# Pairs of chunks as the unit of decay in a linear-attention kernel: states summed in PSUM, weights cast on the way in, k scaled on GpSimd, r copied by stepped PSUM reads

## The chip, the cores and the metric

The kernel runs on one core of a Trainium2 chip. The metric is the device time of one execution in microseconds: 207.22 us for the kernel before (median of 2 runs, 206.41 and 208.04). The profile is of one execution, with a span of 204.4 us from its first to its last instruction.

The core's engines run side by side, each through its own queue in order: TensorE (PE in the profile; PEld is its weight load), VectorE (DVE), ScalarE (ACT), GpSimd (POOL) and SyncE (SP), which here only issues transfers. TensorE writes to PSUM, of which there are eight banks of 512 float32 per partition. VectorE and ScalarE read PSUM and SBUF[...].

## What is computed

Two phases follow each other: a linear attention with per-channel decay, and a token- and channel-mixing block on its output.

```python
# B, H, S, D = 4, 8, 768, 48
for t in range(S):
    kt, vt, rt = k[:, :, t], v[:, :, t], r[:, :, t]
    cur = einsum('bhd,bhe->bhde', u[None] * kt, vt)
    y[:, :, t] = einsum('bhd,bhde->bhe', rt, state + cur)
    state = w[None, :, :, None] * state + einsum('bhd,bhe->bhde', kt, vt)
x = y.transpose(0, 2, 1, 3).reshape(B, S, H * D)      # 4, 768, 384

theta = x @ w_theta
yr = einsum('ts,bsd->btd', w_tok_r, x * cos(theta))
yi = einsum('ts,bsd->btd', w_tok_i, x * sin(theta))
u = x + yr + yi
out = u + maximum(u @ w_ch, 0)
```

## The kernel before

**Chunks.** The 768 tokens of a batch are six chunks of 128 (C), taken in three pairs (`pr`). Within a chunk the decay is put into the operands: r is multiplied by w to a power that rises with the token's place in its chunk (`wpow`), k by one that falls with it (`wpinv`). Then the scores of a chunk are a plain product of k and r, masked to the part below the diagonal, and the state that enters the next chunk is the old state plus the chunk's k-v product, times w to the 128th power (`wC`). The heads go two by two (`hp`, four pairs), each padded from 48 to 64 channels, so that two heads fill 128 partitions.

**`front(b)`** does the attention of a batch and the way to cos and sin.
- r arrives with six consecutive tokens per partition. L397 scales it into `Rw` (GpSimd; for batch 0 two of four head pairs on VectorE). `flip6` transposes six 128x128 blocks into one PSUM bank (L379, TensorE) and ScalarE copies the bank to SBUF as `RT` (L382). Because of the six tokens per partition the copy reads the bank in a row and writes at a step of six elements, so that the tokens come out in order.
- k of a pair of chunks is scaled by VectorE into `Kw` (L416) and transposed to `KT` (L379, L382). v is cast by ScalarE into `vb` (L424).
- Scores of a chunk (L438) fill two banks, one per head of a pair. VectorE masks each into `mAT` (L443). The diagonal with u goes through `PD` (L449), a small product (L459), `dg` (L464) and GpSimd's `yd` (L466).
- The k-v products of the first five chunks (L479) go to PSUM. VectorE adds each to the decayed earlier state, head pair by head pair, into `Y` (L494; a copy for the first, L491), and GpSimd multiplies by `wC` into the bf16 state `Sb` (L499). Both of a chunk's steps hang on the chunk before.
- `outputs` adds state times r (L516) and masked scores times v (L526); VectorE adds `yd` into `x` (L535). x is transposed, multiplied by theta's weights (L552), goes through sin and cos on ScalarE (L556, L559), and becomes `zr` (VectorE, L562) and `zi` (GpSimd, L565).

**`mixing(b)`** multiplies zr and zi of all six chunks by the token weights (twelve matmuls of 384 columns per 128 tokens, L586), adds x (L592), transposes, multiplies by the channel weights (L604), ends with a maximum and an addition (L609) and stores.

**Weights.** Wth and Wch come as float32 and are cast by ScalarE (`square`, L347). Each of twelve row blocks of the token weights comes as float32, is transposed by TensorE in float32, three blocks to a bank (L361), and copied as bf16 by ScalarE (L367). All their transfers, like those of r, k and v, are issued by SyncE, and all but r land in a ring of eight buffers (`ld`). In that queue the weights stand between batch 0's k and v and batch 1's r.

**The order.** Nothing is ordered by hand. `Plan.add` records each step with its engine, an assumed duration, a priority, what it reads and writes and which PSUM banks it takes and gives back. `Plan.order` (L72) plays the list through as a small simulation: at each moment a free engine takes the ready task of the lowest priority number for which banks are free. The kernel is then issued in that order, so assumed durations and priorities fix both the order in each queue and the bank that each result gets. Mixing of a batch has a higher number than the next batch's front, so it fills TensorE's time while the front waits.

Of the kernel before, what the change touches and what calls it, by code (L numbers as in the profile page):

```python
# [19 lines left out]


# [6 lines left out]
PE, DVE, ACT, POOL, SP = "PE", "DVE", "ACT", "POOL", "SP"  # L28


class Task:
    __slots__ = ("eng", "ns", "fn", "deps", "prio", "seq", "lat", "acq", "uses", "nwait",
                 "users", "ready", "end", "mode")


class Plan:
# [3 lines left out]
    def __init__(self, nbanks):  # L40
        self.tasks, self.writer, self.readers = [], {}, {}
        self.nbanks = nbanks
        self.bank_uses = {}
        self.bank_of = {}

    def add(self, eng, ns, fn, rd=(), wr=(), prio=0.0, lat=60.0, acq=(), use=(), mode=None):
        t = Task()
        t.eng, t.ns, t.fn, t.prio, t.lat, t.mode = eng, ns, fn, prio, lat, mode
        t.seq = len(self.tasks)
        t.acq, t.uses = list(acq), list(acq) + list(use)  # L50
        rd, wr = list(rd) + list(use), list(wr) + list(acq)
# [19 lines left out]

    def order(self):  # L72
# [11 lines left out]
        banks = [(0.0, i) for i in range(self.nbanks)]  # L84
# [3 lines left out]
        while len(out) < n:  # L88
            for e in waiting:
                while free_at[e] <= now:  # L90
                    nfree = sum(1 for b in banks if b[0] <= now)
                    best = None
                    for t in waiting[e]:
                        if t.ready <= now and len(t.acq) <= nfree:
                            if best is None or (t.prio, t.seq) < (best.prio, best.seq):
                                best = t
# [4 lines left out]
                    banks.sort()  # L101
                    for b in t.acq:
                        self.bank_of[b] = banks.pop(0)[1]
                    ns = t.ns
                    if e == PE:
                        if t.mode != last_mode:
                            ns += 100.0
                        last_mode = t.mode
                    free_at[e] = now + ns
                    t.end = now + ns + t.lat  # L110
                    out.append(t)
                    for b in t.uses:
                        left[b] -= 1
                        freed[b] = max(freed.get(b, 0.0), t.end)
                        if left[b] == 0:
                            banks.append((freed[b], self.bank_of[b]))
# [7 lines left out]
            nxt += [b[0] for b in banks if b[0] > now]  # L124
# [3 lines left out]
            now = min(nxt)  # L128
        return out


def rows_of(w, n):
    return dataclasses.replace(w, ap=[[0, n]] + [list(x) for x in w.ap])


def wide(ap, n):
    return dataclasses.replace(ap, ap=[list(x) for x in ap.ap] + [[0, n]])
# [3 lines left out]
def kernel(  # L141
# [22 lines left out]
    NS = NCH - 1  # L164
# [4 lines left out]
    bank_t = [ps.tile([C, 512], F32, name=f"bank{i}") for i in range(8)]  # L169

    def bank(tok):
        return bank_t[P.bank_of[tok]]
# [6 lines left out]

# [9 lines left out]
    tok_i = sb.tile([C, NCH + 1], mybir.dt.int32, name="tok_i")  # L189
    tok_f = sb.tile([C, NCH + 1], F32, name="tok_f")  # L190
    wpow = sb.tile([C, H, NCH, D], F32, name="wpow")
    wpinv = sb.tile([C, H, D], F32, name="wpinv")
    wup = sb.tile([C, 2 * HP], F32, name="wup")
    wC = sb.tile([C, HP], F32, name="wC")
    uw = sb.tile([C, HP, 2], BF16, name="uw")

    NL = 8
    Ls = ring(NL, [C, 2 * HD], F32, "ld")
    r_fs = ring(2, [C, H, NCH * D], F32, "r_f")
    Rws = ring(1, [C, NCH, H, Dp], BF16, "Rw")  # L200
    Kws = ring(4, [C, 2, H, Dp], BF16, "Kw")
    vbs = ring(5, [C, 2, H, D], BF16, "vb")
# [3 lines left out]
    mATs = ring(6, [C, 2, HP, C], BF16, "mAT")  # L206
    Ys = ring(1, [C, NS, HP, D], F32, "Y")
    Sbs = ring(2, [C, NS, HP, D], BF16, "Sb")
    dgs = ring(3, [C, 2 * H], F32, "dg")
# [6 lines left out]
    uns = ring(2, [C, 2, HD], BF16, "un")  # L216
# [3 lines left out]
    Wch = sb.tile([C, ND, HD], BF16, name="Wch")  # L220
    WrT = sb.tile([C, NCH, S], BF16, name="WrT")
    WiT = sb.tile([C, NCH, S], BF16, name="WiT")

    def act_ns(n, psum=True):
        return n / 1.2 + (60 if psum else 95)

    def dve_ns(n, rate=1.0):
        return n / (0.96 * rate) + 75

    def pool_ns(n):  # L230
        return 190 + 1.95 * n


    def setup():
        P.add(ACT, 100, lambda: nc.scalar.dma_start(out=w_f, in_=rows_of(w, C)),
              wr=["w_f"], prio=-100, lat=3000)
# [3 lines left out]
        P.add(DVE, 100, wu_fill, wr=["wu"], prio=-100)  # L240

        def wu_load():
            nc.scalar.dma_start(out=wu[:HP, :, :D], in_=w.rearrange("(a b) d -> a b d", b=2))
            nc.scalar.dma_start(out=wu[HP:, :, :D], in_=u.rearrange("(a b) d -> a b d", b=2))
        P.add(ACT, 200, wu_load, wr=["wu"], prio=-99, lat=3000)

        def tok():
            nc.gpsimd.iota(tok_i[:, :NCH], pattern=[[1, NCH]], base=0, channel_multiplier=NCH)
            nc.gpsimd.iota(tok_i[:, NCH:], pattern=[[0, 1]], base=0, channel_multiplier=1)
        P.add(POOL, 400, tok, wr=["tok_i"], prio=-100)  # L250

        def tok2():
            nc.vector.tensor_scalar(tok_i[:, :NCH], tok_i[:, :NCH], C - 1, None,
                                    op0=Alu.bitwise_and)
            nc.vector.tensor_copy(tok_f, tok_i)
            nc.vector.tensor_scalar(tok_f[:, NCH:], tok_f[:, NCH:], -1.0, -1.0,
# [3 lines left out]
        P.add(DVE, 400, tok2, rd=["tok_i"], wr=["tok_f", "uw", "pi2"], prio=-99)  # L260

        def pads(ts):
            for t in ts:
                nc.gpsimd.memset(t[:, :, :, D:], 0.0)
        P.add(POOL, 900, lambda: make_identity(nc, ident_f), wr=["ident_f"], prio=-98)
        P.add(DVE, 200, lambda: nc.vector.tensor_copy(ident, ident_f), rd=["ident_f"],
              wr=["ident"], prio=-98)
        P.add(POOL, 600, lambda: pads(Rws), wr=[("Rw", hp) for hp in range(HP)], prio=-97)
        P.add(POOL, 800, lambda: pads(Kws), wr=[("Kw", i) for i in range(4)], prio=-96)
# [6 lines left out]
        P.add(POOL, 600, mask, wr=["mask"], prio=-95)  # L276
# [383 lines left out]
```

## Time and profile before

| | busy us | share of span | instructions |
|---|---|---|---|
| TensorE matmul | 145.3 | 71% | 1641 |
| VectorE | 124.6 | 61% | 260 |
| ScalarE | 123.3 | 60% | 165 |
| GpSimd | 75.1 | 37% | 73 |

Sums of a line's busy time, in us, for the lines that the change touches:

| line | what | count | us |
|---|---|---|---|
| L382, ACT | all copies after `flip6`, RT (16) among them | 52 | 72.5 |
| L367, ACT | copies of token weights | 24 | 10.2 |
| L397, POOL | r times `wpow` | 14 | 22.7 |
| L416, DVE | k times `wpinv` | 24 | 21.7 |
| L443, DVE | masks | 48 | 30.6 |
| L494, DVE | state update | 80 | 12.5 |
| L499, POOL | state times `wC` | 20 | 11.5 |
| L361, PE | float32 transposes of token weights | 72 | 10.0 |
| L586, PE | token mixing | 288 | 57.9 |

In the profile "RT_104<-bank_65 128x768 bf16<-128x768 bf16" means that the instruction wrote RT, read a PSUM bank, and moved 768 elements on each of 128 partitions. A bracket with an arrow gives the idle time of the engine just before, and what ended it. A busy share is an average over stages with different limits; which engine a stage waits for is read from the stage. TensorE's clock is granted by a throttle and is below full speed in part of the span (mean 0.921).

### The profile page before, as it was taken

The numbers are of one execution on the slowest core, as the hardware profiler recorded it, in microseconds if no ns is written. First come the engines' busy times: TensorE is split into PE (matmuls) and PEld (weight loads), VectorE is DVE, ScalarE is ACT, GpSimd is POOL, SyncE is SP. The second block draws the span as 40 slices with busy tenths as digits, with TensorE's granted clock in tenths as the row PEclk, the third lists the DMA queues.
The fourth block names the chain that finished last, engine by engine and source line by source line (L and its number), as shares of the span: only waits on it lengthen the run. The fifth ranks groups of instructions, "written<-read, shape, count | busy, mean of one in ns | idle before, by whom it ended". The sixth has DMA issues, their size and how long they took to land.

```text
span 204.4 us, 4137 instructions
## 1 busy us (share of the span) xinstructions
PE 145.3 (71%) x1641; PEld 95.7 (47%) x1641; DVE 124.6 (61%) x260; ACT 123.3 (60%) x165; POOL 75.1 (37%) x73
## 2 busy tenths in 40 slices
PE   0008178896582897599933988999329989999971
PEld 0016165774460555356621755657215655566630
DVE  2028279355740899978861999944419896544442
ACT  2299987999599706409999433755992327511120
POOL 6024121606960489523791083440104082400000
PEclk9999999999669589969995899999985999999998
DMA  4999209999899992829290510022020002022222
GB/s 119 236 230 227 112 6 275 333 332 321 170 198 292 189 167 50 263 69 203 81 195 0 129 29 3 0 82 77 0 77 3 0 3 77 3 77 77 79 80 77
DMA packets 60092, 25.25 MB, mean 124 GB/s; under 512 B 50472, under 2 KB 58536, under 8 KB 60072
## 3 DMA queue, kind: packets, MB, share of 16 engines
q1 hardware_dynamic: 59904, 24.78, 49.9%
q8 instruction: 13, 0.21, 0.5%
q10 hardware_dynamic: 168, 0.20, 0.5%
q14 instruction: 7, 0.06, 0.1%
HBM read 20.25 MB, written 4.72 MB: 122 GB/s over the span
## 4 chain that ended last, share of the span: by engine, by line
PE 41%; ACT 21%; DVE 19%; issue 8%; DMA 8%; POOL 1%; ACTq 0%; POOLq 0%; DVEq 0%; SPq 0%
ACT RT_104 L382 8%; ACT RT_105 L382 7%; DMA r_f_93<-in_r_dram 5%; PE bank_66 L586 5%; PE bank_64 L586 3%; DMA wu<-in_u_dram 3%; PE bank_68 L586 2%; PE bank_63 L586 2%; PE bank_65 L586 2%; DVE Y_116 L494 2%; DVE mAT_114 L443 2%; ACT wpow L297 2%; PE bank_67 L586 1%; PE bank_62 L586 1%; DVE Kw_96 L416 1%
## 5 line engine op out<-in xcount | busy, mean ns | idle before, releaser
L586 PEld LDWEIGHTS <-WrT 128*128 128x128 bf16 x144 | 14.5, 104 | 10.4 <-issue 3.1
L499 POOL TENSOR_TENSOR Sb_118<-Y_116,wC 128x192 bf16<-128x192 f32 x10 | 5.4, 544 | 34.0 <-DVE Y_116 L494 18.6
L586 PEld LDWEIGHTS <-WiT 128*128 128x128 bf16 x144 | 12.8, 98 | 6.8 <-issue 0.5
L397 POOL TENSOR_TENSOR Rw_94<-r_f_92,wpow 128x576 bf16<-128x576 f32 x6 | 10.1, 1713 | 10.1 <-ACT wpow L297 10.1
L397 POOL TENSOR_TENSOR Rw_94<-r_f_93,wpow 128x576 bf16<-128x576 f32 x8 | 12.6, 1600 | 0.4 <-DMA r_f_93<-in_r_dram 0.4
L499 POOL TENSOR_TENSOR Sb_117<-Y_116,wC 128x192 bf16<-128x192 f32 x10 | 6.1, 606 | 16.6 <-DVE Y_116 L494 13.5
L379 PEld LDWEIGHTS <-Rw_94 128*128 128x128 bf16 x96 | 8.0, 120 | 8.6 <-issue 6.2
L438 PEld LDWEIGHTS <-KT_107 64*128 64x128 bf16 x96 | 4.1, 116 | 12.4 <-issue 8.1
L449 DVE TENSOR_TENSOR PD_109<-RT_105,KT_107 128x1024 bf16<-128x1024 bf16 x4 | 3.3, 823 | 10.8 <-ACT RT_105 L382 6.6
L449 DVE TENSOR_TENSOR PD_108<-RT_104,KT_106 128x1024 bf16<-128x1024 bf16 x4 | 4.1, 1030 | 6.8 <-ACT KT_106 L382 6.8
L382 ACT ACTIVATE xT_135<-bank_65 128x768 bf16<-128x768 bf16 x2 | 1.6, 810 | 11.0 <-PE bank_65 L379 11.0
L438 PEld LDWEIGHTS <-KT_106 64*128 64x128 bf16 x96 | 3.8, 117 | 8.6 <-ACT KT_106 L382 5.9
L604 PEld LDWEIGHTS <-uT_138 128*128 128x128 bf16 x36 | 3.5, 108 | 8.9 <-ACT uT_138 L382 6.4
L282 PE MATMUL bank_61<-ident_f,wu 8*128 8x8 f32 x1 | 0.2, 239 | 8.7 <-DMA wu<-in_u_dram 8.7
L604 PEld LDWEIGHTS <-uT_139 128*128 128x128 bf16 x36 | 3.2, 98 | 7.0 <-ACT uT_139 L382 5.3
L382 ACT ACTIVATE RT_104<-bank_65 128x768 bf16<-128x768 bf16 x2 | 5.7, 2844 | 0.4 <-PE bank_65 L379 0.4
L382 ACT ACTIVATE RT_104<-bank_63 128x768 bf16<-128x768 bf16 x2 | 5.9, 2946 | 0.0
L382 ACT ACTIVATE RT_105<-bank_66 128x768 bf16<-128x768 bf16 x2 | 5.7, 2842 | 0.1
L604 PE MATMUL bank_68<-Wch,uT_138 128*128 128x384 bf16 x6 | 1.8, 424 | 5.3 <-ACT uT_138 L382 5.3
L379 PE MATMUL bank_62<-ident,Rw_94 128*128 128x128 bf16 x12 | 1.3, 261 | 5.8 <-DVE Rw_94 L397 5.8
L552 PEld LDWEIGHTS <-xT_134 128*128 128x128 bf16 x36 | 3.5, 106 | 4.1 <-ACT xT_134 L382 2.0
L438 PE MATMUL bank_61<-RT_104,KT_106 64*128 64x128 bf16 x12 | 1.4, 246 | 5.6 <-ACT KT_106 L382 5.6
(540 smaller groups left out, 542.3 us busy)
## 6 DMA issues: line engine op xcount, KB each, us to landing
r_f_92<-in_r_dram SPq DMA_DIRECT2D x2, 1152.0 KB, 7.8
r_f_93<-in_r_dram SPq DMA_DIRECT2D x2, 1152.0 KB, 10.4
out_dram<-fin_140 SPq DMA_DIRECT2D x6, 384.0 KB, 2.4
out_dram<-fin_141 SPq DMA_DIRECT2D x6, 384.0 KB, 2.4
ld_88<-in_k_dram SPq DMA_DIRECT2D x4, 192.0 KB, 6.6
ld_89<-in_v_dram SPq DMA_DIRECT2D x4, 192.0 KB, 3.3
ld_84<-in_k_dram SPq DMA_DIRECT2D x4, 192.0 KB, 5.6
ld_87<-in_moe_w_tok_i_dram SPq DMA_DIRECT2D x2, 384.0 KB, 4.6
```

The costliest lines, as they stand in the source:

```text
L297: P.add(ACT, 500 + (1300 if n == 0 else 0), lambda n=n: nc.scalar.activation(wpow[:, :, n, :], lw_f, Act.Exp, scale=tok_f[:, n:n + 1]), rd ...
L379: nc.tensor.matmul(bank16(tok)[:, i * C:(i + 1) * C], s, ident, is_transpose=True, start=(i == 0), stop=(i == n - 1))
L382: P.add(ACT, act_ns(n * C), lambda: nc.scalar.activation(dst, bank16(tok)[:, :n * C].rearrange("p (a c) -> p a c", a=n), Act.Copy), use=[t ...
L397: eng.tensor_mul(Rw[:, :, 2 * hp:2 * hp + 2, :D].transpose([0, 2, 1, 3]), rf[:, 2 * hp:2 * hp + 2, :].rearrange("p h (n d) -> p h n d", n= ...
L438: nc.tensor.matmul(bank(tk[hi])[:, hp * C:(hp + 1) * C], KT[q, c, hp, :], RT[q, hp, cc * C:(cc + 1) * C], start=(hp == 0), stop=(hp == HP ...
L443: P.add(DVE, dve_ns(HP * C), lambda hi=hi, tk=tk, mAT=mAT: nc.vector.tensor_mul(mAT[:, hi], bank(tk[hi]).rearrange("p (h t) -> p h t", h=H ...
L449: nc.vector.tensor_mul(PD, RT[:, :, 2 * pr * C:(2 * pr + 2) * C].rearrange("p h (a t) -> p a h t", a=2), KT)
L494: nc.vector.scalar_tensor_tensor(Y[:, cc, hp, :], Y[:, cc - 1, hp, :], wC[:, hp:hp + 1], src[:, hp], op0=Alu.mult, op1=Alu.add)
L499: P.add(POOL, pool_ns(HP * D), lambda cc=cc: nc.gpsimd.tensor_mul(Sb[:, cc], Y[:, cc], wide(wC, D)), rd=[("Y", cc), "wC"], wr=[("Sb", b % ...
L552: nc.tensor.matmul(bank(th)[:, :HD], xT[:, t, dk, :], Wth[:, dk, :], start=(dk == 0), stop=(dk == ND - 1))
L586: nc.tensor.matmul(bank(tm)[:, :HD], WT[:, so, to * C:(to + 1) * C], z[:, so], start=(part == 0 and j == 0), stop=(part == 3 and j == 2))
L604: nc.tensor.matmul(bank(tf)[:, :HD], uT[:, t, dk, :], Wch[:, dk, :], start=(dk == 0), stop=(dk == ND - 1))
```

## The change

**Decay relative to pairs.** r's power now runs over a pair of chunks (place in the pair minus 128, `wr_t`) and k's likewise (127 minus the place, `wk_t`, one table per chunk of the pair). So the k-v products of a pair's two chunks need no decay between them and add up in PSUM: TensorE forms the first chunk's product (for the state in the middle of the pair) and, beside it, the sum of both (for the state after the pair), at the price of computing the first one twice. VectorE adds the carried state for the middle (`mid`) and for the end (`carry`), over all heads at once. The decay by w to the 256th (`wP`) falls due once per pair: in the first pair on VectorE, in the second on GpSimd (`decay`); ScalarE makes the bf16 copy. It shortens the chain from chunk to chunk.

**r's copies.** `flip6` gets a `view`: ScalarE reads the bank at a step of 128 elements and writes RT in a row. It is meant to move the step from the write to the read.

**k on GpSimd**, chunk by chunk, to relieve VectorE. **Weights cast by their transfer**: issued by GpSimd, they arrive as bf16, in `Wth`, `Wch` and a ring of six row buffers, and are transposed in bf16, six blocks to a bank. ScalarE's casts fall away, and SyncE's queue and ring hold only r, k, v (rings of six chunks each) and the outputs.

**Smaller things.** The PSUM is four tiles of two banks, and scores take an aligned pair of banks, so one mask instruction covers 1024 elements. Ln and exp share one table, loaded early; sin's is loaded early as well. exp no longer waits for the small loads of w and u, which SyncE now issues. The planner's assumed durations are different, and it models the transfers and pairs of banks. Some rings have other sizes (Kw 3, vb 4, mAT 5, un 3).

```diff
+    bank_t = [ps.tile([C, 1024], F32, name=f"bank{i}") for i in range(4)]
...
+        P.add(ACT, 1300, lambda: nc.scalar.preload_act_table_set("natural_log_exp_and_others"),
+              wr=["tab"], prio=-99.5, name="tab")
...
+                P.add(POOL, 1000, lambda row=row, src=src, to=to: nc.gpsimd.dma_start(
+                    out=row, in_=src[to * C:(to + 1) * C, :]), wr=[rk],
+                    prio=prio + to, dma=1100, name=key)
+                flip6(dst[:, :, to * C:(to + 1) * C], [row[:, j * C:(j + 1) * C] for j in range(NCH)],
+                      ("W", key, to), prio + 30 + to, [rk], [(key, to)])
...
-            flip6(RT[:, hp].rearrange("q (p n) -> q n p", n=NCH),
-                  [Rw[:, n, 2 * hp:2 * hp + 2, :] for n in range(NCH)],
-                  ("TR", b, hp), base + hp, [("Rw", hp)], [("RT", b % 2, hp)])
+            flip6(RT[:, hp], [Rw[:, n, 2 * hp:2 * hp + 2, :] for n in range(NCH)],
+                  ("TR", b, hp), base + hp, [("Rw", hp)], [("RT", b % 2, hp)],
+                  view=lambda s: s.rearrange("q (n p) -> q p n", n=NCH))
...
+                P.add(POOL, pool_ns(384, 2.0), lambda c=c, Kw=Kw, ik=ik: nc.gpsimd.tensor_mul(
+                    Kw[:, c, :, :D], lk[ik], wk_t[:, c]),
+                    rd=[("lk", ik), ("wk_t", c)], wr=[kK[c]], prio=pb, name=f"scale_k{b}.{cc}")
...
+                todo = [(0, 0)] if last else [(0, 0), (1, 0), (1, 1)]
+                for a, c in todo:
...
+                            o = (a * HP + hp) * D
                             nc.tensor.matmul(
                                 bank(ts)[hi * Dp:(hi + 1) * Dp, o:o + D], Kw[:, c, h, :],
...
+                    nc.vector.tensor_add(Sb[:, c1], src, Cf[pr % 2])
...
+                        nc.vector.tensor_add(Yf[0][:, 0], src, Cf[pr % 2])
...
+                    P.add(POOL, pool_ns(HP * D), lambda pr=pr: nc.gpsimd.tensor_mul(
+                        Cf[(pr + 1) % 2], Yf[0][:, 0], wide(wP, D)),
```

## The prediction

> **What bounds the kernel now.** I read the page's busy shares and slices first, then the chain, then one window table cut at the places where the chain showed ScalarE, then ScalarE's timeline in one such place, and last the waits of the SyncE queue.
>
> The busy shares, the slices and the chain (on the page; in the slices each digit is a fortieth of the span, 5.1 us):
>
> ```profile
> PE 145.3 (71%) x1641; PEld 95.7 (47%) x1641; DVE 124.6 (61%) x260; ACT 123.3 (60%) x165; POOL 75.1 (37%) x73
> PE   0008178896582897599933988999329989999971
> ACT  2299987999599706409999433755992327511120
> PEclk9999999999669589969995899999985999999998
> GB/s 119 236 230 227 112 6 275 333 332 321 170 198 292 189 167 50 263 69 203 81 195 0 129 29 3 0 82 77 0 77 3 0 3 77 3 77 77 79 80 77
> ...
> ACT RT_104 L382 8%; ACT RT_105 L382 7%; DMA r_f_93<-in_r_dram 5%; PE bank_66 L586 5%; PE bank_64 L586 3%; DMA wu<-in_u_dram 3%; PE bank_68 L586 2%; PE bank_63 L586 2%; PE bank_65 L586 2%; DVE Y_116 L494 2%; DVE mAT_114 L443 2%; ACT wpow L297 2%; PE bank_67 L586 1%; PE bank_62 L586 1%; DVE Kw_96 L416 1%
> ```
>
> TensorE has the most work and is yet idle 204.4 - 145.3 = 59.1 us. Its row dips where ScalarE's is at 9, and its clock digits fall to 5 or 6 near those dips. The chain's two heaviest entries are the copies of the transposed r out of PSUM, RT at L382. The window table puts a number on them. Columns are length, then busy time (and instructions) of PE, PEld, DVE, ACT, POOL, then clock, DMA share and GB/s. The first four rows are the four batches' RT copies, the other four are what lies between them:
>
> ```profile
> 15.00:27.00 12.00, 5.47 (x58) 4.11 (x58) 5.83 (x11) 11.56 (x7) 3.83 (x4) 1.00 0.68 153
> 56.00:67.00 11.00, 5.74 (x44) 3.86 (x43) 2.29 (x4) 11.00 (x10) 3.77 (x3) 0.81 1.17 243
> 99.50:110.00 10.50, 4.06 (x77) 3.32 (x75) 6.15 (x12) 10.50 (x5) 8.27 (x7) 0.87 0.72 131
> 142.50:152.00 9.50, 2.48 (x49) 1.70 (x46) 2.17 (x7) 9.50 (x6) 1.01 (x2) 0.98 0.11 41
> 27.00:56.00 29.00, 23.05 (x310) 18.15 (x311) 20.28 (x41) 24.25 (x48) 13.43 (x11) 0.94 0.87 252
> 67.00:99.50 32.50, 28.63 (x331) 17.66 (x331) 29.52 (x61) 16.21 (x30) 18.29 (x15) 0.85 0.75 145
> 110.00:142.50 32.50, 29.95 (x352) 19.35 (x352) 25.40 (x53) 17.45 (x28) 11.23 (x9) 0.94 0.18 50
> 152.00:204.40 52.40, 45.47 (x428) 27.21 (x428) 30.03 (x63) 15.30 (x27) 11.17 (x9) 0.92 0.12 46
> ```
>
> In the first four ScalarE is full and TensorE idle 6.5 + 5.3 + 6.4 + 7.0 = 25.2 us of 43. In the other four TensorE is idle 6.0 + 3.9 + 2.5 + 6.9 = 19.3 us of 146; before 15 us it does almost nothing. ScalarE's timeline in the third window (start, length) shows why:
>
> ```profile
> 99.31 2.78 ACT L382 ACTIVATE RT_104<-bank_65 128x768 bf16<-128x768 bf16 x1 [0.45 <-PE bank_65 L379]
> 101.70 2.98 ACT L382 ACTIVATE RT_104<-bank_66 128x768 bf16<-128x768 bf16 x1
> 104.29 2.95 ACT L382 ACTIVATE RT_104<-bank_61 128x768 bf16<-128x768 bf16 x1
> 106.85 2.94 ACT L382 ACTIVATE RT_104<-bank_63 128x768 bf16<-128x768 bf16 x1
> 109.40 1.03 ACT L382 ACTIVATE uT_138<-bank_64 128x768 bf16<-128x768 bf16 x1
> ```
>
> uT has the same line, shape and type and takes 1.03 us here, others of that form 0.81. The difference is that RT is written at a step of six elements. And the SyncE queue:
>
> ```profile
> SPq L324 <- ACT Wth L347: 10.2, 1, 10.2
> ```
>
> For 10.2 us a load waits for a landing buffer that ScalarE empties (the theta weights, whose cast stands behind RT). This is the 6 in the GB/s row, slice 6: DMA stands still at 25 to 30 us, and batch 1's r, last in that queue, lands at 51.5.
>
> **What the Trainium skill says.** "ScalarE: Activation LUTs", section "What ACT_TABLE_LOAD costs": an element per cycle whatever the function, 0.833 ns, plus 186 ns per instruction. For 768 elements that is 0.83 us; the trace's 0.81 agrees, and RT at 2.75 to 2.98 does not, so the stepped write is the anomaly. "SBUF — State Buffer", section "Door 1": 16-byte lines in SBUF and 8-byte lines in PSUM, a penalty for crossing; RT's step of 12 bytes fits that for the write, and the changed copy steps 256 bytes in PSUM, for which the page names only matmuls as slowed. No row of before shows a stepped PSUM read. "TensorE: Matmul & The Clock Gate", section "HAM oscillation — how this bites in real kernels": idle gaps over about 3.4 us put TensorE back to a slow clock. The trace agrees: after the RT windows three mixing matmuls take 0.98 to 1.14 us, elsewhere 0.49. "SBUF — State Buffer", section "Who interferes with whom": a VectorE instruction with two SBUF inputs contends with a GpSimd one that reads SBUF. L416 agrees: 0.55 us alone, 1.29 to 1.76 beside the GpSimd scaling of r.
>
> **The change, part by part.**
> RT's 16 copies now read PSUM stepped and write in a row. Bounds: 0.81 us (same shape, in a row both ways) and about 2.85 (if a step costs as much on the read side). I take 0.85, since the per-element figure is for the engine and the slow part here is the two-byte stepped write. ScalarE loses 16 x 2.0 = 32 us, a batch's burst goes from 11.4 to 3.4 us. Of the 25.2 us of TensorE idle in the four windows some 5 stay, because transposes and copies still alternate: -20 us.
>
> Clock. The 288 mixing matmuls take 57.9 us in sum, theta 14.7 and chan 15.5 (72 each). At 0.163 us apiece (0.49 for three) they need 47.0 + 11.7 + 11.7, so 17.7 us are slow clock and lone starts. Fewer long gaps should give back about half: -8.
>
> Head. exp no longer waits for the tiny w and u loads (8.7 us) and a second table load: it began at 10.74 and can follow Ln at 7.65, so 3.1 us earlier. Weights leave the SyncE queue and its landing ring, so the 10.2 us wait is gone and r of batch 1 follows the 12 k and v loads directly. Against that stand the GpSimd's own duties: seven casting loads stand in its queue ahead of the first scaling of r, and k's scaling follows. A casting load's issue time is in no row of before; the lower bound is what SyncE shows, 0.33 us; "DMA: Bandwidth & Descriptors", section "Latency and other measured facts", prices this path at about 1 us to the first byte, the descriptors being made in software. I take 1 and keep 2, its double, as the upper end. So GpSimd is ready at 3.9 + 7 = 10.9, just as exp is done. The loads of batch 0 also share the DMA with 2.9 MB of weights. r (1.2 MB), w (0.2), twelve loads of 0.2 and those weights make 6.7 MB; at the 230 GB/s of slices 2 to 4 that is 29 us, so the last k and v land at about 29, as now (the last v is issued at 29.4). The gain is in what follows: batch 0's last zi ended at 60.1 and should end at about 45. Much of this is the first RT window again, counted above: -4 beyond it.
>
> VectorE. k's 24 multiplies (21.7 us in sum) go to GpSimd. The state update, 16 x 4 small instructions (12.5 us) and four copies (1.4), becomes 12 + 8 of about 0.28 = 5.6. 48 mask multiplies of 0.64 become 24 of about 1.15, half the starts: -3. In all 124.6 - 21.7 - 8.3 - 3 = 92 us. It was the last to end in 74 to 86 us (k beside r): -2.
>
> GpSimd. 75.1 - 11.5 (20 state scalings) + 2.3 (four remain) + 24 k scalings + 14 issues. 192 elements take 0.51, 768 take 1.47: 1.67 ns each, so 384 take 0.83 to 1.1 us, 23 in sum. Total 103 us. It stays below TensorE, but what stands in its queue is now on the way of every front: behind a casting load that waits for its row buffer stand zi and the next batch's k, and KT's transpose waits for these.
>
> TensorE. 72 float32 transposes (9.97 us) become 72 of bf16 at 0.0915 (30.7 / 336) = 6.6; 64 more state products at 0.035 (5.58 / 160) = 2.2. Net -1.2.
>
> Small: ScalarE no longer casts weights (2.8 us) and copies eight states (8 x 0.26), hidden beside TensorE. The two-bank PSUM tiles add no wait of a half for the other, as the order of instructions and waits shows. Scores need a free pair of banks, which costs nothing while masks keep up.
>
> Sum: 204.4 - 20 - 8 - 4 - 2 - 1.2 = 169.2 us of span; the stated time lies 207.2 - 204.4 = 2.8 above the span: 172 us.
>
> **The rivals.**
> Everything packs. TensorE keeps its clock and the fronts hide: 145.3 - 17.7 - 1.2 = 126 of work, 14 of head, 6 of tail (190 to 204 has 5.6 idle), 10 between: 156 + 3 = 159. For it: 170 to 190 us of before is full at a clock of 1.0. Against: only one stretch is so.
>
> GpSimd and the shared DMA take the place of the waits removed. With issue at 2 us, the first scaling starts 7 us later, the six loads of the second half cost 6 more in the middle of batch 1's front, of which half is seen: 172 + 7 + 3 = 182. For it: seven issues ahead of the first useful GpSimd work, and 6 to 10 us from issue to landing in the crowded head. Against: GpSimd idles 63% now.
>
> The stepped read costs what the stepped write did. Then the 20 and 8 stay away: 204.4 - 4 - 2 - 1.2 = 197 + 3 = 200, or about 195 with the DMA hole gone. For it: no row shows such a read. Against: ScalarE is the engine that reads an element per cycle in every other row.
>
> Slower. A stepped read twice as slow as the write adds 11.4 us to each of the four bursts, of which TensorE hides half: 200 + 23 = 223. It needs a cost of 5.7 us for 768 elements, seven times the plain one.
>
> **How the numbers follow.** Forecast 0.56, everything packs 0.08, GpSimd and DMA 0.22, stepped read 0.09, slower 0.05. The likeliest is 172. From 158 to 190 the first three are inside with their scatter, and about 0.16 is left out. Faster by over 2% is below 203: 0.56 + 0.08 + 0.22 and half of the stepped read, 0.05: 0.91. Within 2%: 0.04. Slower: 0.05.
>
> **What would show it.** RT rows of 0.8 to 1.0 us at the new L393; no window with ScalarE full and TensorE under half; no slices at clock 5 or 6 after the head; mixing near 50 us in sum; the last zi of batch 0 near 45 us; no wait of SyncE for a weight cast; VectorE near 92 and GpSimd near 103 us. I am wrong if RT stays above 2 us, if the GpSimd rows of casting loads take over 2 us each or if TensorE's longest idle times are ended by GpSimd's Kw and Rw.

## The result: 195.5 us, and the profile after

The changed kernel takes 195.53 us (median of 2 runs, 194.83 and 196.22), 0.945 of the time before (95% interval 0.931 to 0.959). It is faster, but by 12 us where 35 were forecast.

First the page of the changed kernel: the busy totals, three of the rows of slices that were shown of before, the chain by engine, and the lines of r's copies and of k's multiply.

```profile
PE 140.8 (72%) x1705; PEld 94.0 (48%) x1705; DVE 98.4 (51%) x165; ACT 97.0 (50%) x169; POOL 95.5 (49%) x94
PE   0030369897558889889688899688998788989950
ACT  2750753448947467857784527437715552011110
PEclk9999999999966999999999999999999999999996
...
PE 43%; ACT 22%; DVE 15%; SPq 9%; issue 6%; DMA 1%; POOL 1%; DVEq 0%; ACTq 0%; POOLq 0%
...
L393 ACT ACTIVATE RT<-bank 128x768 bf16<-128x768 bf16 x16 | 12.9, 811 | 10.2 <-PE bank L386 6.5
L427 POOL TENSOR_TENSOR Kw<-lk,wk_t 128x384 bf16<-128x384 f32 x24 | 24.0, 1014 | 8.3 <-DMA lk<-in_k_dram 8.2
```

What was meant to happen to single instructions did happen. A copy of RT takes 811 ns in place of 2.85 us, so ScalarE is at half load. Of the slices of before at clock 5 or 6 two are left, at 53 to 63 us, besides the last of the span. What is odd is TensorE's row. Three other engines stand at about 50%, and TensorE's digits after the head are 8 and 9 and hardly ever a run of 9: it is nowhere starved for long and nowhere full. The chain says the same: 43% TensorE, then ScalarE with 22% and VectorE with 15%.

Windows of before (first) and after, cut at 60 and 140 us (columns: window, length, then busy time and instructions of PE, PEld, DVE, ACT, POOL, clock, DMA share, GB/s):

```profile
0.00:60.00 60.00, 32.79 (x393) 25.47 (x393) 30.83 (x66) 47.36 (x72) 25.06 (x32) 0.94 0.84 214
60.00:140.00 80.00, 62.04 (x736) 39.07 (x736) 60.86 (x124) 49.08 (x62) 37.88 (x31) 0.89 0.56 115
```

```profile
0.00:60.00 60.00, 30.04 (x372) 22.50 (x373) 21.44 (x37) 32.41 (x57) 36.24 (x49) 0.95 1.03 203
60.00:140.00 80.00, 68.47 (x950) 46.38 (x948) 51.19 (x84) 50.19 (x89) 50.16 (x41) 0.99 0.43 96
```

In the first 60 us TensorE gets less done than before, with a DMA that is busy all the time (share 1.03). From 60 to 140 it is still idle 11.5 us of 80, at a clock of 0.99, with no other engine above 64%. Waits make that up, and they are many and short. From the waits of the changed kernel (engine, line that waits, what released it, us in sum, times, longest):

```profile
PE bank L386 <- ACT RT L393: 3.6, 5, 1.3
PE bank L613 <- ACT uT L393: 2.5, 4, 1.2
PE bank L613 <- ACT xT L393: 1.4, 2, 0.9
...
ACT uT L393 <- PE bank L386: 20.2, 4, 5.4
ACT uT L393 <- PE bank L613: 7.7, 3, 3.6
...
DVE un L622 <- PE bank L613: 7.4, 8, 2.2
DVE un L622 <- PE bank L634: 6.0, 2, 3.0
```

Two of these name a releaser that the waiting step has no business with. `uT` is copied from what the transposes of L386 wrote, yet 7.7 us of its waits end with a token-mixing matmul (L613). `un` reads the mixing's bank, yet 6.0 us of its waits end with a channel matmul (L634). TensorE's timeline shows the same at one place, and ScalarE's beside it (start, length):

```profile
94.40 0.49 PE L386 MATMUL bank<-ident,Rw 128*128 128x128 bf16 x6 [0.41 <-ACT RT L393]
...
97.28 0.49 PE L386 MATMUL bank<-ident,un 128*128 128x128 bf16 x6 [0.39 <-ACT RT L393]
```

```profile
93.54 0.81 ACT L393 ACTIVATE RT<-bank 128x768 bf16<-128x768 bf16 x1
...
96.42 0.81 ACT L393 ACTIVATE RT<-bank 128x768 bf16<-128x768 bf16 x1 [0.68 <-DVE un L622]
```

The transposes of `un` start right after a copy of RT ends (96.42 + 0.81 = 97.23). They need `un` and a free bank, not RT; and that copy of RT, in its turn, had stood 0.68 us until VectorE was done with `un`. Either the bank was the one just copied, or something ties it to that copy. The experiments had to tell these apart.

### The profile page after: what moved, and what is told of

Same layout as the page of the kernel before. It is cut to its first block, busy times and chain, and to the rows that moved or that the text cites. A ratio compares the mean times of both kernels' runs of the same rounds, so it can differ in the third digit from the quotient of the medians.

```text
span 194.5 us, 4151 instructions
## 1 busy us (share of the span) xinstructions
PE 140.8 (72%) x1705; PEld 94.0 (48%) x1705; DVE 98.4 (51%) x165; ACT 97.0 (50%) x169; POOL 95.5 (49%) x94
## 4 chain that ended last, share of the span: by engine, by line
PE 43%; ACT 22%; DVE 15%; SPq 9%; issue 6%; DMA 1%; POOL 1%; DVEq 0%; ACTq 0%; POOLq 0%
PE bank L613 18%; PE bank L386 9%; SPq L358 8%; PE bank L634 4%; PE bank L579 4%; ACT bank L586 3%; ACT xT L393 3%; DVE mAT L456 3%; ACT KT L393 3%; ACT uT L393 3%; DVE zr L589 3%; ACT RT L393 3%; PE bank L451 3%; DVE x L562 3%; ACT sin L583 2%
## 5 line engine op out<-in xcount | busy, mean ns | idle before, releaser
L613 PE MATMUL bank<-zi,WiT 128*128 128x384 bf16 x144 | 30.8, 325 | 4.2 <-DVE fin L639 0.9
L613 PE MATMUL bank<-zr,WrT 128*128 128x384 bf16 x144 | 28.9, 325 | 6.4 <-ACT uT L393 2.1
L592 POOL TENSOR_TENSOR zi<-x,sin 128x768 bf16<-128x768 bf16 x12 | 20.0, 1664 | 26.6 <-ACT sin L583 25.3
L456 DVE TENSOR_TENSOR mAT<-bank,mask 128x1024 bf16<-128x1024 f32 x24 | 28.6, 1212 | 2.2 <-PE bank L451 2.2
L427 POOL TENSOR_TENSOR Kw<-lk,wk_t 128x384 bf16<-128x384 f32 x24 | 24.0, 1014 | 8.3 <-DMA lk<-in_k_dram 8.2
L622 DVE TENSOR_TENSOR un<-bank,x 128x384 bf16<-128x384 f32 x24 | 13.1, 553 | 21.9 <-PE bank L613 7.4
L406 POOL TENSOR_TENSOR Rw<-r_f,wr_t 128x576 bf16<-128x576 f32 x14 | 21.5, 1544 | 3.8 <-ACT wr_t L330 2.2
L479 POOL TENSOR_TENSOR yd<-dg,vb 128x768 bf16<-128x768 f32 x12 | 17.7, 1474 | 11.0 <-ACT dg L477 10.9
L613 PEld LDWEIGHTS <-WrT 128*128 128x128 bf16 x144 | 13.6, 97 | 16.2 <-issue 8.3
L386 PE MATMUL bank<-ident,Rw 128*128 128x128 bf16 x96 | 10.0, 257 | 14.9 <-DVE Rw L406 11.8
L613 PEld LDWEIGHTS <-WiT 128*128 128x128 bf16 x144 | 12.9, 97 | 12.8 <-issue 6.4
L579 PE MATMUL bank<-Wth,xT 128*128 128x384 bf16 x72 | 15.9, 359 | 1.8 <-ACT xT L393 1.5
L386 PEld LDWEIGHTS <-Rw 128*128 128x128 bf16 x96 | 8.1, 116 | 17.2 <-issue 15.3
L634 PE MATMUL bank<-Wch,uT 128*128 128x384 bf16 x72 | 14.3, 326 | 1.8 <-ACT uT L393 1.0
```

The costliest lines, as they stand in the source:

```text
L386: nc.tensor.matmul(bank16(tok)[:, i * C:(i + 1) * C], s, ident, is_transpose=True, start=(i == 0), stop=(i == n - 1))
L406: eng.tensor_mul(Rw[:, :, 2 * hp:2 * hp + 2, :D].transpose([0, 2, 1, 3]), rf[:, 2 * hp:2 * hp + 2, :].rearrange("p h (n d) -> p h n d", n= ...
L427: P.add(POOL, pool_ns(384, 2.0), lambda c=c, Kw=Kw, ik=ik: nc.gpsimd.tensor_mul(Kw[:, c, :, :D], lk[ik], wk_t[:, c]), rd=[("lk", ik), ("wk ...
L456: P.add(DVE, dve_ns(2 * HP * C), lambda tk=tk, mAT=mAT: nc.vector.tensor_mul(mAT.rearrange("p i h t -> p (i h) t"), bank(tk, 2).rearrange( ...
L479: P.add(POOL, pool_ns(2 * HD), lambda yd=yd, dg=dg, vb=vb: nc.gpsimd.tensor_mul(yd.rearrange("p a h d -> p (a h) d"), wide(dg, D), vb.rear ...
L579: nc.tensor.matmul(bank(th)[:, :HD], xT[:, t, dk, :], Wth[:, dk, :], start=(dk == 0), stop=(dk == ND - 1))
```

## The experiments

Each run stands beside runs of the kernel before on the same chip, and the ratio in brackets is to those, with its 95% interval. These runs of before took 206.3 to 206.8 us, so a difference between runs on two chips carries about half a microsecond.

### Which half of the change: the stepped read alone, and all but it

e0_after is the changed kernel itself. e1 adds the stepped read to the kernel before, e2 takes it out of the changed one; no instruction moves in either.

```diff
-            flip6(RT[:, hp].rearrange("q (p n) -> q n p", n=NCH),
-                  [Rw[:, n, 2 * hp:2 * hp + 2, :] for n in range(NCH)],
-                  ("TR", b, hp), base + hp, [("Rw", hp)], [("RT", b % 2, hp)])
+            flip6(RT[:, hp], [Rw[:, n, 2 * hp:2 * hp + 2, :] for n in range(NCH)],
+                  ("TR", b, hp), base + hp, [("Rw", hp)], [("RT", b % 2, hp)],
+                  view=lambda s: s.rearrange("q (n p) -> q p n", n=NCH))
```

> The changed kernel unaltered, as the yardstick of this chip for the runs beside it. All theories: 194 to 197 us, with TensorE waiting about 22 us before microsecond 30, 16 us between 60 and 180.

> The kernel before, with one edit: the sixteen copies of r's transposed blocks write a plain row and step through PSUM instead; the order on every engine is that of before. Theory C (the prediction's: the bursts of these copies are worth 28 us in idle TensorE and slow starts): 179 us. Theory A (the copies were worth about 10 us after microsecond 60, and the rest of what the windows lost is bound by the supply of k and v at the head): 193 to 198 us. Theory B (TensorE loses its time to short groups and short waits that no copy sets): 197 to 203 us. In all three a copy takes 0.81 us in place of 2.85.

> The changed kernel with that one edit taken back: r's copies write with a step of six again; the same order on every engine. ScalarE gains 16 x 2.04 = 33 us of work. Theory C: plus 28 us, 223 us. Theories A and B: plus 10 to 15 us, 205 to 210 us, since the other parts of the change brought little.

Measured: e0 194.75 us (0.945, 0.940 to 0.950), e1 180.46 us (0.874, 0.869 to 0.880), e2 222.85 us (1.081, 1.074 to 1.088). So theory C, the prediction's own, holds for this term: minus 26.0 us in the old surroundings, and plus 28.1 us when it is taken out of the new. Theories A and B, formed from the changed kernel's trace, fall. The page of e1:

```profile
PE 137.9 (77%) x1641; PEld 91.4 (51%) x1641; DVE 125.2 (70%) x260; ACT 95.1 (53%) x165; POOL 75.4 (42%) x73
```

TensorE's idle time is 178.8 - 137.9 = 40.9 us against 59.1 before, so 18.2 less, and its busy time is 7.4 less. These are the prediction's 20 and 8. The surprise is the other side of it: **all the rest of the change costs 194.75 - 180.46 = 14.3 us**, where it was forecast to bring 7.

### The head

e3: the tiny loads of w and u are issued by ScalarE, right behind its own load, instead of by SyncE behind the first v. (The diff leaves out the two lines taken from SyncE.)

```diff
             nc.scalar.dma_start(out=w_f, in_=rows_of(w, C))
+            nc.scalar.dma_start(out=wu[:HP, :, :D], in_=w.rearrange("(a b) d -> a b d", b=2))
+            nc.scalar.dma_start(out=wu[HP:, :, :D], in_=u.rearrange("(a b) d -> a b d", b=2))
```

> The changed kernel with the two small loads of w and u issued by ScalarE right behind its own load of w, rather than by SyncE behind the first v pair; all else in the same order. Theory A: the flips of r's parts 0 and 2 no longer stand behind a weight transpose that waits for these loads, the 7.3 us wait goes, first scores come 2 to 4 us earlier and the whole ends 3 to 7 us earlier, 189 to 192 us. Theory B, and any theory that k's arrival at 17.6 us bounds the head: 0 to 1.5 us earlier.

Measured: 194.88 us (0.945, 0.939 to 0.951), nothing gained. TensorE's timeline of e3 shows why:

```profile
14.50 0.27 PE L317 MATMUL bank<-ident_f,wu 8*128 8x8 f32 x1
15.03 0.80 PE L388 MATMUL bank<-ident,Rw 128*128 128x128 bf16 x6 [0.26 <-DVE wup L321]
21.93 0.80 PE L388 MATMUL bank<-ident,Rw 128*128 128x128 bf16 x6 [6.10 <-ACT RT L395]
```

The transpose of w and u comes 6.2 us earlier (20.73 in the changed kernel), and then the fourth transposition of r stands 6.1 us until ScalarE has copied the third one. One wait took the place of another, and again it is TensorE waiting for a copy. The third and the fourth transposition fill the two halves of one pair of banks, and the third copy stands in ScalarE's queue behind casts of v, whose data land at about 19.5 us.

f1: the first seven weight loads go behind the fourth multiply of k in GpSimd's queue; all else keeps its place.

```diff
+        if t.name in ("Wth", "WrT", "WiT") and t.eng == POOL and held is not None:
+            held.append(t)
+            continue
...
+        if t.name == "scale_k0.3":
+            todo += held
```

> The changed kernel with the first seven weight loads moved, in GpSimd's queue, from ahead of r's scaling to behind the fourth multiply of k; every other instruction keeps its place. Seen so far: the kernel before with the stepped read alone takes 180.5 us, so the other parts of the change cost 14 us, and its first scores start at 20.9 us against 27.0 in the changed kernel, where the third and fourth chunk of k land at 21 to 22.5 us. Theory H (the early weight loads take the DMA time that k and v need, and that costs the 6 us of the head): first scores at about 22 us, the whole 4 to 7 us shorter, 188 to 191 us. Theory O (the loss sits in the order of TensorE's work after microsecond 60): within 1.5 us of 194.8.

Measured: 190.40 us (0.922, 0.919 to 0.926). Theory H holds for its 4.4 us. GpSimd's timeline of the changed kernel and then of f1:

```profile
17.63 0.99 POOL L427 TENSOR_TENSOR Kw<-lk,wk_t 128x384 bf16<-128x384 f32 x1 [3.83 <-DMA lk<-in_k_dram]
18.84 0.99 POOL L427 TENSOR_TENSOR Kw<-lk,wk_t 128x384 bf16<-128x384 f32 x1 [0.22 <-DMA lk<-in_k_dram]
22.60 2.04 POOL L427 TENSOR_TENSOR Kw<-lk,wk_t 128x384 bf16<-128x384 f32 x2 [2.77 <-DMA lk<-in_k_dram]
```

```profile
14.94 3.85 POOL L427 TENSOR_TENSOR Kw<-lk,wk_t 128x384 bf16<-128x384 f32 x4
```

With the weights out of the way, four chunks of k are there when GpSimd is; with them in the way GpSimd waits three times. SyncE's queue shows why k's second pair is late. The first pair of v holds it for 11.17 us in the changed kernel, as the last section shows, and for less than half of that in f1:

```profile
4.94 5.03 SPq L358 DMA_DIRECT2D lv<-in_v_dram  x2
```

So k's second pair is issued at 11.56 us in place of 19.47. The first scores begin at 22.4 us, against 27.0 in e0 and 28.0 in the profile shown above. The gain is a third of the 14 us; the miss after 60 us is another matter.

### The order, and the engine of k

f2 gives the planner the durations that TensorE's steps have in the trace (five steps, two of them shown), and nothing extra for a change of kind.

```diff
-        P.add(PE, 56 * n, go, rd=rd + ["ident"], acq=[tok], prio=prio, mode=0, name=f"flip{tok}")
+        P.add(PE, 91 * n, go, rd=rd + ["ident"], acq=[tok], prio=prio, mode=0, name=f"flip{tok}")
...
-            P.add(PE, 720, outputs, rd=rt_keys + mk + kv_ + [
+            P.add(PE, 1020, outputs, rd=rt_keys + mk + kv_ + [
```

> The changed kernel with the planner told what TensorE's steps took on the chip: 91 ns a transposed block in place of 56, 420 a scores step in place of 210, 720 the outer products in place of 400, 350 the diagonal in place of 210, 1020 the outputs in place of 720, and nothing extra for a change of kind. Only the order of the work on the engines differs. Theory O (the planner, told too short times, orders TensorE's work so that it waits for results that are not there yet; 12 us of idle time between 80 and 160 against 6 us in the kernel before with the stepped read): 4 to 8 us shorter, 187 to 191 us. Theory H: within 2 us of 194.8.

Measured: 202.18 us (0.979, 0.972 to 0.985), 7.4 us longer. Theory O, that too short assumed times spoil the order, is refuted in this form: the order made with measured times was worse. Why it was worse was not followed up, and it was tried only with the pairs of banks in place.

e5 issues k's multiplies to VectorE, at the same place.

```diff
-                P.add(POOL, pool_ns(384, 2.0), lambda c=c, Kw=Kw, ik=ik: nc.gpsimd.tensor_mul(
+                P.add(POOL, pool_ns(384, 2.0), lambda c=c, Kw=Kw, ik=ik: nc.vector.tensor_mul(
```

> The changed kernel with k's 24 multiplies issued to VectorE again, at the same place in the program's order. GpSimd loses 24.0 us, VectorE gains about 22 us (0.92 us each in the kernel before). If GpSimd's queue is what costs (k scaled late behind r and the weight loads, r of the next batch behind k): 3 to 6 us shorter, 189 to 192 us. If the queue costs nothing and VectorE's relief is worth what the prediction took (2 us): 196 to 200 us.

Measured: 203.54 us (0.984, 0.979 to 0.990), 8.8 us longer and above both ranges. GpSimd's queue is not what costs, and moving k there was right, by more than the 2 us given to it.

### The banks

f3 declares PSUM as eight tiles of one bank, as before the change. The scores then take two banks one by one and are masked by two multiplies.

```diff
-    bank_t = [ps.tile([C, 1024], F32, name=f"bank{i}") for i in range(4)]
+    bank_t = [ps.tile([C, 512], F32, name=f"bank{i}") for i in range(8)]
...
-                tk = ("A", b, cc)
+                tk = [("A", b, cc, hi) for hi in range(2)]
...
+                for hi in range(2):
+                    P.add(DVE, dve_ns(HP * C), lambda tk=tk, mAT=mAT, hi=hi: nc.vector.tensor_mul(
+                        mAT[:, hi], bank(tk[hi]).rearrange("p (h t) -> p h t", h=HP),
+                        bc(mask01, 1, HP)),
```

> The changed kernel with PSUM held as eight tiles of one bank instead of four of two, and the scores masked by two multiplies of 512 columns instead of one of 1024, as before the change; the planner orders the work anew. Theory P (pairs of banks make TensorE wait: a mask of 1.2 us holds two banks, and a step in one half waits for a reader of the other): 5 to 9 us shorter, 186 to 190 us, with the waits of TensorE on VectorE's and ScalarE's reads in mid kernel gone, though VectorE has 24 times 0.14 us more to do. Theories H and O: within 2 us of 194.8.

Measured: **167.94 us** (0.812, 0.807 to 0.817), 26.8 us less than the changed kernel. Even theory P had expected 5 to 9 us, so its price was far too low. From the page of f3, its windows, and its waits:

```profile
PE 130.9 (78%) x1705; PEld 89.3 (53%) x1705; DVE 98.5 (59%) x189; ACT 93.8 (56%) x169; POOL 96.9 (58%) x94
PE   0011067839745999999999999999999999999960
```

```profile
0.00:60.00 60.00, 29.99 (x427) 22.47 (x428) 23.96 (x49) 35.27 (x62) 40.12 (x51) 0.91 1.06 203
60.00:140.00 80.00, 79.22 (x1133) 53.71 (x1131) 63.83 (x121) 53.04 (x99) 55.17 (x43) 1.00 0.44 99
```

```profile
ACT uT L392 <- PE bank L385: 18.8, 6, 4.4
...
DVE un L623 <- PE bank L614: 9.7, 9, 2.2
```

The head is as slow as in the changed kernel (30.0 us of work by 60), but from 60 to 140 TensorE is busy 79.2 us of 80, a row of nines. `uT` now waits for its own transposes only and `un` for the mixing only. Three things differ between f3 and the changed kernel, though: the declaration, the width of the mask, and the order that the planner makes with it. g1 is f3 with only the declaration taken back, in f3's order on every engine and with f3's bank numbers:

```diff
-    bank_t = [ps.tile([C, 512], F32, name=f"bank{i}") for i in range(8)]
+    bank_t = [ps.tile([C, 1024], F32, name=f"bank{i}") for i in range(4)]
...
-        return bank_t[i]
+        o = 512 * (i % 2)
+        return bank_t[i // 2][:, o:o + 512]
```

> The eight-bank version (168 us) with one thing taken back: PSUM is declared as four tiles of two banks again. Planner, bank numbers, masks and the order on every engine stay the same. Theory P1 (the waits are between the two halves of a declared pair: a write to one half is held until the reads of the other half issued before it are done): 187 to 196 us, with TensorE's waits on ScalarE's and VectorE's reads of PSUM back in mid kernel. Theory P2 (the wide mask and the planner's rule for aligned pairs of banks cost the 27 us): 167 to 171 us.

Measured: 199.93 us (0.969, 0.964 to 0.974), 32.0 us above f3 and 4 above P1's range. It is the declaration. The planner's aligned pairs and the wide mask are not the harm: the changed kernel, which has both, is 5.2 us faster than g1. One and the same stretch of TensorE's order, in g1 and then in f3:

```profile
96.22 0.65 PE L615 MATMUL bank<-zi,WiT 128*128 128x384 bf16 x3
...
104.16 0.61 PE L386 MATMUL bank<-ident,Kw 128*128 128x128 bf16 x8 [0.37 <-DVE mAT L457]
...
112.89 0.65 PE L581 MATMUL bank<-Wth,xT 128*128 128x384 bf16 x3 [0.49 <-DVE mAT L457]
...
116.63 0.38 PE L545 MATMUL bank<-Sb,RT 64*128 64x48 bf16 x16 [0.69 <-DVE zr L591]
...
118.95 0.65 PE L615 MATMUL bank<-zr,WrT 128*128 128x384 bf16 x3
```

```profile
84.49 0.65 PE L614 MATMUL bank<-zi,WiT 128*128 128x384 bf16 x3
...
97.97 1.31 PE L580 MATMUL bank<-Wth,xT 128*128 128x384 bf16 x6
...
102.85 0.65 PE L614 MATMUL bank<-zi,WiT 128*128 128x384 bf16 x3
103.34 0.65 PE L614 MATMUL bank<-zr,WrT 128*128 128x384 bf16 x3
```

From the start of the first row to that of the last it is 22.7 us in g1 and 18.9 in f3. The six matmuls of theta run as one piece of 1.31 us in f3; in g1 the last three start apart, after a wait for a mask that reads PSUM. A break can cost more than its wait. A piece of three is listed at 0.65 us, yet the next one starts 0.49 us after it where nothing holds it (102.85 and 103.34), so its end, which otherwise lies under the next piece, stands alone when TensorE has to wait. Over the span TensorE is idle 197.8 - 140.7 = 57.1 us in g1 and 167.5 - 130.9 = 36.6 in f3, and its busy time, for the same matmuls, is 9.8 us longer in g1. How much of the 9.8 such ends make up was not worked out.

The compiled program shows the ties. TensorE's first instructions in the changed kernel, with their waits (weight loads left out):

```
Matmult bank_61<-ident,Rw_94 128x128
...  (six in all: the first transposition of r, first bank of the pair)
Matmult bank_61<-ident,Rw_94 128x128 [waits Activation_49]
...  (the second, into the second bank of the pair)
```

In f3 the same second transposition goes to bank_62 and that matmul has no such wait. What such a tie costs shows at the third and fourth transposition. In the changed kernel the fourth waits until a copy ends, that of the third by ScalarE's timeline (22.07 to 22.88 us); in f3 both run as one piece of twelve. The rows of the changed kernel, then of f3:

```profile
21.23 0.80 PE L386 MATMUL bank<-ident,Rw 128*128 128x128 bf16 x6 [0.26 <-DVE wup L319]
22.93 0.80 PE L386 MATMUL bank<-ident,Rw 128*128 128x128 bf16 x6 [0.90 <-ACT RT L393]
```

```profile
20.96 1.46 PE L385 MATMUL bank<-ident,Rw 128*128 128x128 bf16 x12
```

So it is the program that makes a write to one half wait for a read of the other half: where both are one declared tile, the framework orders the accesses to it as if they touched. The waits of `uT` for token mixing are the other direction, a read of one half held by a write to the other.

g2 tries the width of the mask alone: each mask of 1024 columns as two of 512 in the same place, pairs kept.

```diff
+                    for hi in range(2):
+                        nc.vector.tensor_mul(
+                            mAT[:, hi],
+                            bank(tk, 2)[:, 512 * hi:512 * hi + 512].rearrange("p (h t) -> p h t", h=HP),
+                            bc(mask01, 1, HP))
```

> The changed kernel with each mask of 1024 columns issued as two of 512 in the same place, everything else in the same order and in pairs of banks. Theory P1: 194 to 197 us, VectorE 1.5 to 3 us busier. Theory P2, if the width of the mask is what costs: 175 to 190 us.

Measured: 195.72 us (0.948, 0.942 to 0.955), no difference from the changed kernel. The wide mask is neither the harm nor, by itself, a gain.

h2 puts the declaration of pairs into the kernel before with the stepped read (e1); no instruction moves.

```diff
-    bank_t = [ps.tile([C, 512], F32, name=f"bank{i}") for i in range(8)]
+    bank_t = [ps.tile([C, 1024], F32, name=f"bank{i}") for i in range(4)]
...
-        return bank_t[P.bank_of[tok]]
+        i = P.bank_of[tok]
+        o = 512 * (i % 2)
+        return bank_t[i // 2][:, o:o + 512]
```

> The kernel before with the stepped read (180.5 us), and PSUM declared as four tiles of two banks instead of eight of one; no instruction moves. Theory P1: 195 to 210 us, as the waits come to this kernel too. Theory P2, or the declaration of pairs costing only in the changed order: 180 to 183 us.

Measured: 211.28 us (1.024, 1.018 to 1.030), 30.8 us above e1 and 1 above P1's range, and so slower than the kernel before in spite of the stepped read. ScalarE's waits in e1 and then in h2:

```profile
ACT uT L385 <- PE bank L379: 23.2, 9, 4.5
```

```profile
ACT uT L387 <- PE bank L381: 16.5, 7, 4.8
...
ACT uT L387 <- PE bank L590: 12.7, 3, 5.4
```

The foreign releaser of `uT` (L590 is token mixing there) appears with the pairs, with nothing else changed. A foreign releaser alone is no proof, though: with single banks e1 has one as well, at the copies of `xT`:

```profile
ACT xT L385 <- DVE mAT L445: 9.9, 2, 5.7
```

### The other terms, once the banks are single

i1 is f3 with the stepped write of RT (e2's edit), i2 is f3 with k on VectorE (e5's edit).

> The eight-bank version (168 us) with r's copies writing at a step of six again; same order on every engine. If the prediction's terms for r's copies (20 us of idle TensorE and 8 us of slow starts) hold once the pairs of banks are gone: 194 to 198 us. If the pairs had been part of what made a slow copy dear (the copies of one half holding up the other): 178 to 186 us.

> The eight-bank version with k's 24 multiplies issued to VectorE at the same place in the program. With pairs of banks the same edit cost 8.8 us (203.6 against 194.8), for 22 us more of VectorE's work. If moving k to GpSimd is worth the 2 us that the prediction gave VectorE's relief: 169 to 171 us. If it is worth more because TensorE waits for k's multiplies behind the masks in VectorE's queue: 173 to 178 us.

Measured: i1 192.76 us (0.937, 0.930 to 0.943), 24.8 us above f3; i2 175.04 us (0.848, 0.846 to 0.851), 7.1 us above. i1 lands just under its first range and well above the second, so the copies of r are worth 25 to 28 us with or without pairs. i2's windows show what k's move does:

```profile
60.00:140.00 80.00, 74.90 (x1082) 50.28 (x1082) 69.40 (x128) 51.21 (x95) 38.64 (x27) 1.00 0.44 96
```

VectorE is busy 69.4 us of 80 here, against 63.8 in f3, and TensorE loses 4.3 us in that stretch. From e1 to f3, that is for all of the change but r's copies and the pairs, the time falls by 12.5 us. k's move is 7.1 of it; the decay by pairs, from which the change has its title, and the weights cast on the way in were not run apart.

### A version that beats both

h1 is f3 with both repairs of the head (f1's and e3's edits), and r of batch 2 loaded behind batch 1's k.

```diff
+        if t.name == "ld_r2":
+            r2 = t
+            continue
...
+        if r2 is not None and t.name == "ld_lk1.5":
+            todo.append(r2)
```

> The eight-bank version with three repairs of the head: the first seven weight loads stand behind the fourth multiply of k in GpSimd's queue, the small loads of w and u are issued by ScalarE ahead of everything in SyncE's queue, and r of batch 2 is loaded after batch 1's k. If the head is bound by the DMA's supply (TensorE idle 33 us of the first 60 in the eight-bank version): 160 to 165 us. If TensorE's work after the head only moves earlier into waits for later loads: 166 to 169 us.

Measured: 164.03 us (0.795, 0.791 to 0.799). Its first window:

```profile
0.00:60.00 60.00, 35.60 (x535) 26.40 (x536) 32.35 (x60) 37.27 (x68) 45.56 (x56) 0.97 1.09 209
```

This is within the first range. TensorE does 5.6 us more by 60 us than in f3, and 3.9 us of it reach the end. The three repairs were not run apart here. The earlier w and u, which brought nothing in e3, meet no tied half here: the third and fourth transposition of r follow at once, where the fourth had stood 6.1 us:

```profile
14.66 1.46 PE L387 MATMUL bank<-ident,Rw 128*128 128x128 bf16 x12
```

## Why the prediction was wrong

**The step that failed** is one sentence among the small things: that the two-bank tiles "add no wait of a half for the other, as the order of instructions and waits shows". They do add such waits, worth 32.0 us in one order (g1 less f3) and 30.8 in another (h2 less e1). For the kernel as planned the step from pairs to single banks, with the planner's new order, brought 26.8 us (f3). The listing already showed it: both halves carry the name bank_61, so a wait for the copy of the other half reads like the plain wait for a bank's own copy, and one has to ask which half each instruction means. No rival covered it; all of them put the loss on an engine or on the DMA. The rival with the slow stepped read named about 195 us, close to the measured 195.5, but that is chance: its cause did not come true. Nor did the three signs of being wrong that the prediction had named.

**r's copies: right.** The row is 811 ns where 850 was taken. The gain is 26.0 us in sum (e1), against 20 + 8, and the split holds: 18.2 idle, 7.4 busy. In the changed kernel the 20 seemed to have shrunk, since TensorE was idle only 5.4 us less than before (53.7 against 59.1); that was the pairs' loss laid over it. The two traces alone had suggested theory A, which e1 overturned.

**Clock: right in sum, wrong in its place.** Token mixing was to fall to about 50 us and is 56.4 in the changed kernel, 55.5 in e1, 54.9 in f3, where the clock from 60 to 140 us is 1.00. So much of what was booked as slow clock and lone starts stays at full clock: the 0.163 us apiece is the distance from start to start, while a piece of three is listed at 0.65 us, and it is this that the 1.14 us of a slow one compares with. Only some 3.6 of the 7.4 us of busy time came from mixing, theta and channel matmuls (88.2 us before, 84.6 in e1). That all of the 7.4 is the clock is not shown. The idle time of about 3.4 us that the prediction took to bring the slow clock fits the 5.32 us before 110.48 in the kernel before; but there three mixing matmuls also take 0.65 us at 61.28 and 1.12 at 68.62, with two waits of only 2.3 us between them.

**The head, -4: failed.** First scores began at 27.0 us before and 28.0 after. The prediction saw that 6.7 MB share the DMA and put k and v at 29 us "as now", but did not price that k's second pair would come later than before: it was issued at 9.83 us before and at 19.47 after, behind v in SyncE's queue. Moving the weights out of the way brought 4.4 us (f1). The last zi of batch 0 was to end near 45 us and ended at 61.6; in h1 it ends at 50.9. A casting load's issue time, taken as 1 us, is 0.93 us for three row blocks and 0.55 for one, so seven take 4.3 us and not 7. GpSimd was in fact ready before exp, waiting 2.2 us for it, so the time that the issues took in its queue cost nothing; what the loads cost was the DMA's time.

**VectorE, -2: too small.** With k on VectorE f3 takes 7.1 us more (i2), the changed kernel 8.8 (e5). VectorE's sum came to 98.4 us, not 92: the wide mask takes 1.21 us, not 1.15, which is 1.5 us of that; the rest was not followed up. GpSimd's 95.5 is below the 103.

Without the pairs, then, the change takes 167.9 us (f3), 4 us from the forecast of 172. The copies brought 26.0 us where 28 were taken, all else 12.5 (f3 less e1) where 7.2 were. That this is so close is partly luck, since the missing gain of the head and the larger one of k's move offset each other. What the forecast lacked was the 26.8 us of the pairs.

## What to carry to other kernels

Declare PSUM by the unit that is handed over, here the bank, and not by the widest thing that someone reads: a tile of two banks saves 24 instruction starts and ties every two banks into one resource. In a profile the signs are waits whose releaser the waiting step doesn't read, and an engine row of eights where no engine is full; they raise the suspicion, and the declaration changed alone settles it. When several edits come together, add the strongest to the old kernel and take it out of the new one first: two runs split the account, where the two traces alone misled.

## What the runs showed of the hardware

- A ScalarE copy that reads 768 bf16 elements from PSUM at a step of 128 elements and writes a row takes 811 ns in the changed kernel, as a copy in a row does there (810, `uT`); the same copy with a write to SBUF at a step of six elements takes 2771 ns (e2).
- A pair of loads of v with runs of 192 bytes held SyncE's queue for 11.17 us in the changed kernel, whose seven weight loads share the DMA at that time, with two 1.5 KB loads standing behind it. It was 5.03 us in f1, where the weight loads come later:

```profile
6.71 11.17 SPq L358 DMA_DIRECT2D lv<-in_v_dram  x2
17.92 0.82 SPq L273 DMA_DIRECT2D wu<-in_w_dram  x1
```

- k's multiply of 384 elements takes 0.74 us on VectorE in the mean (e5) and 1.01 on GpSimd in the changed kernel, and in this kernel it belongs on the slower of the two (e5, i2).
- Three mixing matmuls are listed at 0.65 us, and the next three start 0.49 us after them where nothing holds them (f3). So 0.65 - 0.49 = 0.16 us at the end of a piece lies under the next one, and is added to a wait that breaks the run. This is an estimate from the listed times, in which the ends of matmuls are modelled.
